# The first router's logits of three token tiles in one stage, their products in turn on three column tiles

## The chip, the cores and the metric

One core of a Trainium2 chip runs the whole program in one launch. The metric is the device time of a run in microseconds; of several runs the median counts. Lower is better.

## The reference

A chunked attention feeds two mixture-of-experts layers, each of which sends a token to the one expert with the largest logit. The change touches the first layer's logits alone.

```
out = softmax(q_c @ k_c.T / 8) @ v_c            # 4 x 8 x 9 chunks of 64 tokens, head size 64
x = out, heads side by side: 2304 tokens x 512
logits = x @ w_gate + modality_bias[modality_id] # 512 x 8: the first router
e = argmax(logits); gate = softmax(logits)[e]
x = gate * (relu(x @ w1[e]) @ w2[e])             # 512 x 1024 x 512, 8 experts
... the second layer: the same with a capacity of 576 tokens per expert
```

## The kernel before, in words

The 2304 tokens are 18 tiles of 128. The program has two parts that overlap a little: attention with the first router, tile by tile, and then 37 expert blocks of up to 128 tokens each, in two layers.

A tile t of attention passes these stages (`tile_ops`, L767 to L829); the letters are used from here on:

- S (TensorE, L778): scores of 8 heads, 16 products of 64 x 64. The two halves of the partitions take turns, so one product reads rows 0 to 63 and writes columns 0 to 63 of the array, the next rows and columns 64 to 127.
- maximum and subtraction (VectorE, L781, L783), exp (ScalarE, L784).
- T (TensorE, L789): four transposes; copy by ScalarE (L791).
- O (TensorE, L798): 16 products with v, in turns as in S.
- the norm (VectorE, three instructions, L804 to L806) writes the tile's rows x into one of four buffers `xr`; a store sends them to HBM (SyncE, L808). A norm so waits until the store of four tiles earlier has left its buffer.
- X (TensorE, L813): four transposes of x; copy by ScalarE into a buffer of `tr` (L815).
- E (TensorE, L821): the router's logits, transposed: four products, with 32 columns of `wgs1` (8 of them experts) as weights and 128 tokens as the moving side, summed in 32 partitions of bank L. Tile j of a group writes partitions 32 j to 32 j + 31, which is column tile j of the array.
- after the last E of a group, once for the group: a copy lt (ScalarE, L825), a transpose F (TensorE, L827), and the addition of the bias into `lg` (VectorE, L828). Groups have 3, 3, 4, 4 and 4 tiles (`LGROUPS`).

The first two groups (six tiles) feed an early routing on VectorE, some 60 small instructions, with ranking (L346, L348), index (L491) and gate (L516) products on TensorE. It chooses the first five blocks. Its table `row1a` tells SyncE which expert's weights to load (`weights`, L553). All 18 tiles feed the second routing, which runs beside the first blocks.

A block gathers its tokens (GpSimd, L617), transposes them (TX, L636), and runs two layers (L649, L678) with float32 split in two parts. The weights are converted into these parts by ScalarE (L597: high part), VectorE and GpSimd (L599: low part). Those of block 0 go into the memory that held the rings of q and k. So their conversion starts only once S of tile 17 is done. The gather of block 0 and its first matmul need no other tile of attention; the stages of tiles 14 to 17 stand around them in the queues.

The order on each engine is fixed when the program is built. A planner takes operations with engine, cost and priority, and simulates their start times; each engine then runs its queue in order. Priority is by tile and stage: tile t's stage d has t + 0.7 d, lower first.

Of the kernel before, what the change touches and what calls it, by code (L numbers as in the profile page):

```python
# [20 lines left out]
P = 128  # L21
NTOK = 2304
NT = NTOK // P
H = 8
HD = 64
D = 512
E = 8
FF = 1024
DC = D // P
# [26 lines left out]
GROUPS = [1, 1] + [2] * 8  # L56
GMAX = 2
RING = 4
LGROUPS = [3, 3, 4, 4, 4]
NB, NX = 3, 4  # L60

MARGIN = 1.0
# [8 lines left out]
class Planner:  # L71
# [14 lines left out]
    def op(self, eng, cost, fn, r=(), w=(), after=(), prio=(MAIN, 0.0), lat=0.1, dma=0.0, name=""):  # L86
        o = Op()
        o.eng = eng if isinstance(eng, dict) else {eng: cost}
        o.fn, o.prio, o.lat, o.dma, o.name = fn, prio, lat, dma, name
        o.margin = 0.0  # L90
        deps = set(after)
        for k in r:
            deps |= set(self.wr.get(k, ()))
        for k in w:
            deps |= set(self.wr.get(k, ())) | set(self.rd.get(k, ()))
        for k in r:
            self.rd.setdefault(k, []).append(o)
        for k in w:
            self.wr[k], self.rd[k] = [o], []
        deps.discard(o)  # L100
        o.deps = deps
        o.n = len(self.ops)
        self.ops.append(o)
        return o
# [54 lines left out]
def kernel(ctx, tc, q, k, v, ids, cap, cst, wg1, bias, w1a, w2a, wg2, w1b, w2b, out):  # L159
    nc = tc.nc  # L160
    V, A, PE, SP, G = nc.vector, nc.scalar, nc.tensor, nc.sync, nc.gpsimd
# [5 lines left out]
    op = plan.op  # L167

    def sb(shape, name, dt=F32, tag=None):
        return cp.tile(shape, dt, name=name, tag=tag or name)  # L170
# [13 lines left out]
    wgs1 = sb([P, DC, 32], "wgs1")  # L184
# [14 lines left out]
    stg1 = [sb([P, DC, FF], f"stg1_{i}") for i in range(2)]  # L199
    stg2 = [sb([P, FC, D], f"stg2_{i}") for i in range(2)]  # L200
    RW = GMAX * H * HD
    big = [sb([P, max(DC * FF, n)], f"big{i}") for i, n in enumerate((RING * RW, RING * RW, RING * GMAX * H * (HD + 1), 6 * 512))]
    qr = big[0][:, 0:RING * RW].rearrange("p (r g a c x) -> p r g a c x", r=RING, g=GMAX, a=4, c=2)
    kr = big[1][:, 0:RING * RW].rearrange("p (r g a c x) -> p r g a c x", r=RING, g=GMAX, a=4, c=2)
    vr = big[2][:, 0:RING * GMAX * H * (HD + 1)].rearrange("p (r g h x) -> p r g h x", r=RING, g=GMAX, h=H)
    tr = big[3][:, 0:6 * 512].rearrange("p (i x) -> p i x", i=6)
    lt = big[3][:, 3072:3200]
    bt1 = big[3][:, 3200:3200 + NT * E].rearrange("p (t e) -> p t e", e=E)
    wv = [None] * 4

    def take(which):
# [5 lines left out]
        return wv[k].rearrange("p (c f) -> p c f", c=(DC, FC)[k // 2])  # L217

    RINGS = [tuple(f"{n}{r}" for r in range(RING)) for n in "qkv"]
    TRS = tuple(f"tr{i}" for i in range(6))  # L220

    WKEYS = ("w1",) + RINGS[0] + RINGS[1], ("w2", "lt", "bt1") + RINGS[2] + TRS

# [530 lines left out]
    where = [(g, j) for g, n in enumerate(GROUPS) for j in range(n)]  # L754
    lwhere = [(n, j) for n in LGROUPS for j in range(n)]
    halves = [slice(0, HD), slice(HD, P)]
# [11 lines left out]
    def tile_ops(t):  # L768
        g, j = where[t]
        r_ = g % RING  # L770
        pr = [(MAIN, t + 0.7 * d - 100) for d in range(5)]
        S = bank[f"A{t % 2}"].rearrange("p (c x) -> p c x", x=HD)
        a, b, c4 = t % 2, 2 + t % 2, 4 + t % 2

        def stA():
            for hc in range(8):
# [24 lines left out]
        rr, x, kx = arr[t % 2], xr[t % NX], f"xr{t % NX}"  # L801
# [7 lines left out]
        X = bank["X"]  # L809
# [2 lines left out]
            for c in range(DC):  # L812
                PE.transpose(X[:, c * P:(c + 1) * P], x[:, c * P:(c + 1) * P], ident)  # L813
        op("PE", 0.44, stD, r=[kx], w=["X"], prio=pr[3], lat=0.25, name=f"X{t}")
        op("A", 0.5, lambda: A.copy(tr[:, c4, :], X), r=["X"], w=[f"tr{c4}"], prio=pr[3], name=f"xt{t}")  # L815
        n, jl = lwhere[t]
        Lb = bank["L"]

        def stE():
            for c in range(DC):  # L820
                PE.matmul(Lb[32 * jl:32 * jl + 32, 0:P], lhsT=wgs1[:, c, :], rhs=tr[:, c4, c * P:(c + 1) * P], start=(c == 0), stop=(c == DC - 1))  # L821
        op("PE", 0.4, stE, r=[f"tr{c4}"], w=["L"], prio=pr[4], lat=0.25, name=f"E{t}")
        if jl == n - 1:
            r, t0 = slice(0, 32 * n), t - jl
            op("A", 0.18, lambda: A.copy(lt[r], Lb[r, 0:P]), r=["L"], w=["lt"], prio=pr[4], name=f"lt{t}")  # L825
            Tv = Lb[:, 256:256 + 32 * n].rearrange("p (a b) -> p a b", b=32)
            op("PE", 0.11, lambda: PE.transpose(Lb[:, 256:256 + 32 * n], lt[r], ident[r, r]), r=["lt"], w=["L"], prio=pr[4], lat=0.25, name=f"F{t}")  # L827
            lgops.append((t, op("V", 0.2, lambda: V.tensor_add(lg[:, t0:t0 + n, :], Tv[:, :, 0:E], bt[:, t0:t0 + n, :]), r=["L", "bt"], prio=pr[4], name=f"lgt{t}")))  # L828
# [36 lines left out]
    for t in range(NT):  # L865
        if where[t][1] == 0 and where[t][0] >= RING:
            load(where[t][0])
        if t == 2:
            op("V", 1.8, prep_small, r=["small"], w=["bt", "bt1"], after=[plan.ops[-1]], prio=(SIDE, 0))
        tile_ops(t)  # L870
# [75 lines left out]
```

## Time and profile before

| what | us |
|---|---|
| median of 3 runs | 620.72 (619.61 to 621.53) |
| the profiled execution: its time | 616.94 |
| its span, first to last instruction | 615.2 |
| TensorE busy | 570.2 |
| VectorE, ScalarE, GpSimd busy | 410.2, 254.8, 268.0 |
| granted clock of TensorE, mean | 0.982 of 2.4 GHz |

The profiled execution is one run, 3.8 us under the median of the timed ones. A row of the timeline merges instructions of one kind that follow each other; xN counts recorded instructions. A float32 product is recorded as two of them. What stands in brackets is idle time of the engine before the row and what ended it. A matmul's recorded duration contains its way through the array, so durations of successive rows overlap; the distance from start to start is what a stage takes.

### The profile page before, as it was taken

The numbers are of one execution on the slowest core, as the hardware profiler recorded it, in microseconds if no ns is written. First come the engines' busy times: TensorE is split into PE (matmuls) and PEld (weight loads), VectorE is DVE, ScalarE is ACT, GpSimd is POOL, SyncE is SP. The second block draws the span as 40 slices with busy tenths as digits, with TensorE's granted clock in tenths as the row PEclk, the third lists the DMA queues.
The fourth block names the chain that finished last, engine by engine and source line by source line (L and its number), as shares of the span: only waits on it lengthen the run. The fifth ranks groups of instructions, "written<-read, shape, count | busy, mean of one in ns | idle before, by whom it ended". The sixth has DMA issues, their size and how long they took to land. (4 is left out here: it accounts for less than half of the span.)

```text
span 615.2 us, 11859 instructions
## 1 busy us (share of the span) xinstructions
PE 570.2 (93%) x4026; PEld 460.6 (75%) x4026; DVE 410.2 (67%) x730; ACT 254.8 (41%) x439; POOL 268.0 (44%) x193
## 2 busy tenths in 40 slices
PE   7999999999999999999897989797999999999991
PEld 6888887778778787878686867686887767786770
DVE  2667675956675466776998885871349897776750
ACT  2444455334343343334344545242426664464430
POOL 3000231354443343433655564182248687645630
PEclk9999999999999999999997999898999999999997
DMA  8977940021423151243144345016565954767000
GB/s 297 409 252 257 385 152 11 0 71 54 138 81 111 39 156 35 58 173 104 69 156 137 114 154 154 31 39 221 166 236 222 336 178 150 259 239 261 14 32 15
DMA packets 44418, 91.78 MB, mean 149 GB/s; under 512 B 7396, under 2 KB 16676, under 8 KB 44208
## 3 DMA queue, kind: packets, MB, share of 16 engines
q1 hardware_dynamic: 38208, 72.13, 33.7%
q0 software_dynamic: 6128, 18.69, 9.0%
q8 instruction: 35, 0.57, 0.4%
q14 instruction: 47, 0.39, 0.2%
HBM read 181.72 MB, written 19.29 MB: 327 GB/s over the span
## 5 line engine op out<-in xcount | busy, mean ns | idle before, releaser
L649 PE MATMUL bankA<-wv,xh 128*128 128x512 f32 x592 | 151.7, 407 | 3.9 <-DVE wv L579 3.0
L696 DVE SCALAR_TENSOR_TENSOR junk<-xr,wgb 128x512 f32<-128x512 f32 x112 | 104.4, 932 | 57.9 <-ACT xr L681 51.9
L649 PEld LDWEIGHTS bankA<-wv,xh 128*128 128x128 f32 x592 | 110.3, 192 | 30.9 <-DVE wv L579 5.6
L579 DVE TENSOR_TENSOR wv<-stg,wv 128x1024 fp32r<-128x1024 f32 (+1 forms) x60 | 125.3, 2139 | 2.6 <-ACT wv L587 2.6
L579 POOL TENSOR_TENSOR wv<-stg,wv 128x1024 fp32r<-128x1024 f32 (+1 forms) x40 | 103.5, 2609 | 40.2 <-DVE wv L584 26.4
L690 POOL TENSOR_TENSOR junk<-xr,wgb 128x512 f32<-128x512 f32 x40 | 60.6, 1519 | 45.9 <-ACT xr L681 45.0
L678 PE MATMUL bankX<-wv,hh 128*128 128x512 f32 x288 | 72.2, 400 | 5.7 <-ACTq L606 3.0
L649 PE MATMUL bankA<-wv,xl 128*128 128x512 f32 x296 | 75.9, 396 | 0.1
L659 ACT ACTIVATE h<-bankA 128x512 f32<-128x512 f32 x74 | 42.3, 593 | 64.7 <-PE bankA L649 64.5
L678 PEld LDWEIGHTS bankX<-wv,hh 128*128 128x128 f32 x288 | 52.7, 188 | 19.4 <-DVE wv L579 4.4
L649 PEld LDWEIGHTS bankA<-wv,xl 128*128 128x128 f32 x296 | 55.2, 188 | 13.8 <-issue 0.6
L587 ACT CAST wv<-stg 128x1024 fp32r<-128x1024 f32 x60 | 59.0, 1049 | 1.2 <-ACT r_ex L364 0.4
L678 PE MATMUL bankL<-wv,hid 128*128 128x512 f32 x216 | 52.8, 399 | 1.4 <-ACTq L606 0.8
L667 PE MATMUL bankO<-ident,h 128*128 128x128 f32 x296 | 45.5, 284 | 7.6 <-ACT h L659 7.2
L691 ACT ACTIVATE junk<-junk 128x512 f32<-128x512 f32 x40 | 25.3, 633 | 58.3 <-POOL junk L690 58.2
L667 PEld LDWEIGHTS bankO<-ident,h 128*128 128x128 f32 x296 | 34.3, 144 | 19.8 <-ACT h L659 15.2
L678 PEld LDWEIGHTS bankL<-wv,hid 128*128 128x128 f32 x216 | 39.8, 188 | 11.1 <-ACTq L606 1.3
L670 DVE TENSOR_TENSOR hl<-bankO,hh 128x512 fp32r<-128x512 f32 x56 | 36.4, 679 | 7.0 <-ACT hh L669 6.9
L670 DVE TENSOR_TENSOR hid<-bankO,hid 128x512 fp32r<-128x512 f32 x18 | 12.1, 686 | 41.6 <-ACT hid L669 36.2
L678 PE MATMUL bankL<-wv,hh 128*128 128x512 f32 x160 | 39.5, 399 | 0.0
L701 POOL DMA_INDIRECT xs<-xr,sidx1b x14 | 15.8, 1126 | 50.0 <-DVEq L606 24.3
L640 DVE TENSOR_TENSOR xl<-bankT,xh 128x512 fp32r<-128x512 f32 x37 | 25.4, 687 | 17.5 <-ACT xh L639 14.3
(203 smaller groups left out, 726.2 us busy)
## 6 DMA issues: line engine op xcount, KB each, us to landing
stg<-in_w1a SPq DMA_DIRECT2D x19, 2048.0 KB
stg<-in_w2a SPq DMA_DIRECT2D x19, 2048.0 KB
stg<-in_w1b SPq DMA_DIRECT2D x18, 2048.0 KB
stg<-in_w2b SPq DMA_DIRECT2D x18, 2048.0 KB
xs<-xr SPq DMA_DIRECT2D x18, 260.0 KB
out<-zero SPq DMA_DIRECT2D x3, 1536.0 KB
big<-in_v SPq DMA_DIRECT2D x8, 520.0 KB
big<-in_q SPq DMA_DIRECT2D x8, 512.0 KB
```

Source lines behind the costliest of these rows:

```text
L579: eng.tensor_sub(lo[:, a:b], s[:, a:b], hi.bitcast(F32)[:, a:b])
L587: A.copy(hi[:, c * FF:(c + 1) * FF], s[:, c * FF:(c + 1) * FF])
L640: op("V", 0.61, lambda: V.tensor_sub(xl[j], Tv, xh[j].bitcast(F32)), r=["T", f"xh{j}"], w=[f"xl{j}"], prio=soon, name=f"xl{i}")
L649: PE.matmul(bank[f"A{n}"], lhsT=lhs[j][:, c, :], rhs=w[:, c, n * 512:(n + 1) * 512], start=(k == 0 and c == 0), stop=(k == 2 and c == DC - 1))
L659: op("A", 0.5, lambda n=n: A.activation(h[:, n, :], bank[f"A{n}"], AF.Relu), r=[f"A{n}"], w=[f"h{n}"], prio=main, name=f"relu{i}")
L667: PE.transpose(On[:, f * P:(f + 1) * P], h[:, n, f * P:(f + 1) * P], ident)
L670: op("V", 0.61, lambda r=r, Ov=Ov: V.tensor_sub(hid[hb][1][:, r, :], Ov, hid[hb][0].bitcast(F32)[:, r, :]), r=[f"O{n}", f"hh{n}{alt}"], w= ...
L678: PE.matmul(Y, lhsT=hid[hb][lhs][:, f, :], rhs=wview(w)[:, f, :], start=(k == 0 and f == 0), stop=(k == 2 and f == FC - 1))
L690: op("G", 1.25, lambda e=e, m=m: G.tensor_mul(junk[m], x1[:, 0:D], wgb[:, e, :]), r=[kx, "wgb"], w=[f"junk{m}"], prio=lp, name=f"lg{i}")
L691: op("A", 0.5, lambda e=e, m=m: A.activation(junk[m], junk[m], AF.Copy, accum_out=x1[:, D + e:D + e + 1]), r=[f"junk{m}"], w=[kx + "A"], p ...
L696: V.scalar_tensor_tensor(junk[0], in0=x1[:, 0:D], scalar=1.0, in1=wgb[:, e, :], op0=ALU.mult, op1=ALU.mult, accum_out=x1[:, D + e:D + e + 1])
L701: G.indirect_dma_start(out=dst, out_offset=bass.IndirectOffsetOnAxis(ap=tab.sidx[:, b:b + 1], axis=0), in_=x1[:, 0:w], in_offset=None, bou ...
```

## The change

- `LGROUPS` becomes six groups of three tiles.
- E is no longer a stage of each tile but of a group: it is issued once, after X of the group's third tile, with all 12 products. The loop over the four chunks is outside, the loop over the three tiles inside, so successive products go to column tiles 0, 1, 2, 0, 1, 2 and so on. The planner's cost for it is 1.1 us, for three former stages of 0.4.
- The transposed x of the three tiles must lie side by side until then: `tr` has seven buffers of 512 where it had six, and three of them, not two, hold transposed x.
- lt, F and the addition come six times, not five, always for three tiles.

```diff
-LGROUPS = [3, 3, 4, 4, 4]
+LGROUPS = [3] * 6
...
-    tr = big[3][:, 0:6 * 512].rearrange("p (i x) -> p i x", i=6)
-    lt = big[3][:, 3072:3200]
+    tr = big[3][:, 0:7 * 512].rearrange("p (i x) -> p i x", i=7)
+    lt = big[3][:, 3584:3712]
...
-        a, b, c4 = t % 2, 2 + t % 2, 4 + t % 2
+        a, b = t % 2, 2 + t % 2
+        n, jl = lwhere[t]
+        c4 = 4 + jl
...
         def stE():
             for c in range(DC):
-                PE.matmul(Lb[32 * jl:32 * jl + 32, 0:P], lhsT=wgs1[:, c, :], rhs=tr[:, c4, c * P:(c + 1) * P], start=(c == 0), stop=(c == DC - 1))
-        op("PE", 0.4, stE, r=[f"tr{c4}"], w=["L"], prio=pr[4], lat=0.25, name=f"E{t}")
+                for k in range(n):
+                    src = tr[:, 4 + k, :]
+                    PE.matmul(Lb[32 * k:32 * k + 32, 0:P], lhsT=wgs1[:, c, :], rhs=src[:, c * P:(c + 1) * P], start=(c == 0), stop=(c == DC - 1))
         if jl == n - 1:
+            op("PE", 1.1, stE, r=[f"tr{4 + k}" for k in range(n)], w=["L"], prio=pr[4], lat=0.25, name=f"E{t}")
```

The planner then puts the stages of attention in another order. In the changed program S is L781, T L792, O L801, X L816, E L825 and F L831.

TensorE in the middle of attention, from T of tile 2 on. Before:

```order
L789 MATMUL bankT<-ident,big_100 128x128 x4
L821 MATMUL bankL<-big_100,wgs_80 32x128 x4
L778 MATMUL bankA_66<-big_98,big_97 64x64 x16
L813 MATMUL bankX<-ident,xr_104 128x128 x4
L798 MATMUL bankO<-big_99,big_100 64x65 x16
```

TensorE, now, a little later: from O of tile 3 to X of tile 3.

```order
L801 MATMUL bankO<-big_99,big_100 64x65 x16
L825 MATMUL bankL<-big_100,wgs_80 32x128 x12
L792 MATMUL bankT<-ident,big_100 128x128 x4
L831 MATMUL bankL<-ident,big_100 128x96
L816 MATMUL bankX<-ident,xr_106 128x128 x4
```

E stood in each tile's turn with 4 products; now it stands in every third turn with 12.

TensorE from the last S (tile 17) to the expert blocks. Before, it is the first row, with X of tile 14 ahead of it:

```order
L778 MATMUL bankA_67<-big_98,big_97 64x64 x16
L798 MATMUL bankO<-big_99,big_100 64x65 x16
L789 MATMUL bankT<-ident,big_100 128x128 x4
L821 MATMUL bankL<-big_100,wgs_80 32x128 x4
L813 MATMUL bankX<-ident,xr_106 128x128 x4
L798 MATMUL bankO<-big_99,big_100 64x65 x16
L789 MATMUL bankT<-ident,big_100 128x128 x4
L821 MATMUL bankL<-big_100,wgs_80 32x128 x4
L636 MATMUL bankT<-ident,xb_107 128x128 x4
L813 MATMUL bankX<-ident,xr_103 128x128 x4
L798 MATMUL bankO<-big_99,big_100 64x65 x16
L821 MATMUL bankL<-big_100,wgs_80 32x128 x4
```

TensorE now, from the last S on:

```order
L781 MATMUL bankA_67<-big_98,big_97 64x64 x16
L792 MATMUL bankT<-ident,big_100 128x128 x4
L816 MATMUL bankX<-ident,xr_105 128x128 x4
L801 MATMUL bankO<-big_99,big_100 64x65 x16
L825 MATMUL bankL<-big_100,wgs_80 32x128 x12
L792 MATMUL bankT<-ident,big_100 128x128 x4
L831 MATMUL bankL<-ident,big_100 128x96
L816 MATMUL bankX<-ident,xr_106 128x128 x4
L801 MATMUL bankO<-big_99,big_100 64x65 x16
L636 MATMUL bankT<-ident,xb_107 128x128 x4
L816 MATMUL bankX<-ident,xr_103 128x128 x4
L801 MATMUL bankO<-big_99,big_100 64x65 x16
```

Both end with TX of block 1 and block 0's first matmul behind what is shown. X of tile 14 (`xr_105`), T of tile 16 and F have moved behind the last S, and three E have become one.

VectorE from the two passes over tile 17's scores on; `wv` is a conversion of block 0's weights, `xr` a norm's last step. Before:

```order
L781 TENSOR_REDUCE amx_125<-bankA_67 128x8
L783 TENSOR_TENSOR big_100<-bankA_67,amx_125 128x512
L804 TENSOR_SCALAR arr_127<-bankO 128x8
L805 RECIPROCAL arr_127<-arr_127 128x8
L806 TENSOR_TENSOR xr_106<-bankO,arr_127 128x512
L599 TENSOR_TENSOR wv_1355<-stg_0_93,wv_1354 128x1024 x2
L804 TENSOR_SCALAR arr_126<-bankO 128x8
L805 RECIPROCAL arr_126<-arr_126 128x8
L806 TENSOR_TENSOR xr_103<-bankO,arr_126 128x512
L599 TENSOR_TENSOR wv_1355<-stg_0_93,wv_1354 128x1024
L640 TENSOR_TENSOR xl_112<-bankT,xh_110 128x512
```

VectorE now, from the same place:

```order
L784 TENSOR_REDUCE amx_125<-bankA_67 128x8
L786 TENSOR_TENSOR big_100<-bankA_67,amx_125 128x512
L807 TENSOR_SCALAR arr_126<-bankO 128x8
L808 RECIPROCAL arr_126<-arr_126 128x8
L809 TENSOR_TENSOR xr_105<-bankO,arr_126 128x512
L599 TENSOR_TENSOR wv_1322<-stg_0_93,wv_1321 128x1024
L807 TENSOR_SCALAR arr_127<-bankO 128x8
L808 RECIPROCAL arr_127<-arr_127 128x8
L809 TENSOR_TENSOR xr_106<-bankO,arr_127 128x512
L599 TENSOR_TENSOR wv_1322<-stg_0_93,wv_1321 128x1024
L832 TENSOR_TENSOR lg<-bankL,bt 128x24
L599 TENSOR_TENSOR wv_1322<-stg_0_93,wv_1321 128x1024
```

Norm 14 (`xr_105`) has come behind the last scores, norm 16 (`xr_103`) now follows only behind the last row shown, and an addition into `lg` stands between the conversions.

SyncE around the first weight loads: `xs<-xr_105` is the store of tile 10. Before:

```order
L808 DMA xs<-xr_104 128x520
L872 DMA wgb<-in_wg 128x4096
L808 DMA xs<-xr_105 128x520
L565 TENSOR_LOAD row1a
L565 ISA x2
L553 ISA
L553 DMA stg_0_93<-in_w1a 128x4x1024
```

SyncE now, at the fourth weight issue:

```order
L566 TENSOR_LOAD row1a
L566 ISA x2
L553 ISA
L553 DMA stg_1_96<-in_w2a 128x8x512
L811 DMA xs<-xr_105 128x520
L811 DMA xs<-xr_106 128x520
```

The store of tile 10 has moved from ahead of the four weight issues to behind them.

## Rows read from the trace of the kernel before

**Rows 1.** The page, engines: busy us (share of span) and recorded instructions

```profile
PE 570.2 (93%) x4026; PEld 460.6 (75%) x4026; DVE 410.2 (67%) x730; ACT 254.8 (41%) x439; POOL 268.0 (44%) x193
```

**Rows 2.** Busy time by stage: length, engines' busy us, granted clock, DMA

```profile
20.00:80.00 60.00, 60.00 (x1138) 51.10 (x1138) 40.09 (x128) 26.27 (x48) 4.61 (x7) 1.00 0.87 319
```

**Rows 3.** Timeline of TensorE, one tile's turn: start us, us, instruction, count

```profile
23.98 1.06 PE L821 MATMUL bankL<-big,wgs 128*32 128x128 f32 x8
24.98 1.15 PE L778 MATMUL bankA<-big,big 64*64 64x64 f32 x32
26.05 0.65 PE L813 MATMUL bankX<-ident,xr 128*128 128x128 f32 x4
...
27.72 0.66 PE L789 MATMUL bankT<-ident,big 128*128 128x128 f32 x4
28.30 1.06 PE L821 MATMUL bankL<-big,wgs 128*32 128x128 f32 x8
```

**Rows 4.** By line, 0 to 95 us: busy us, mean ns, idle before

```profile
L778 PEld LDWEIGHTS bankA<-big,big 64*64 64x64 f32 x576 | 18.3, 134 | 6.5 <-issue 6.3 <-DMA big<-in_v 0.2
...
L821 PE MATMUL bankL<-big,wgs 128*32 128x128 f32 x136 | 18.0, 276 | 0.0
L821 PEld LDWEIGHTS bankL<-big,wgs 128*32 128x32 f32 x136 | 13.5, 109 | 2.6 <-issue 1.7 <-ACT big L784 0.8
```

**Rows 5.** Timeline of TensorE, 24.96 to 25.00 us alone

```profile
24.77 0.27 PE L821 MATMUL bankL<-big,wgs 128*32 128x128 f32 x1
24.98 0.27 PE L778 MATMUL bankA<-big,big 64*64 64x64 f32 x2
```

**Rows 6.** Timeline of TensorE, last S to block 0's first matmul

```profile
78.28 1.15 PE L778 MATMUL bankA<-big,big 64*64 64x64 f32 x32
...
86.28 0.66 PE L813 MATMUL bankX<-ident,xr 128*128 128x128 f32 x4 [0.23 <-DVE xr L806]
...
88.94 0.66 PE L636 MATMUL bankT<-ident,xb 128*128 128x128 f32 x4
89.35 3.98 PE L649 MATMUL bankA<-wv,xh 128*128 128x512 f32 x16
```

**Rows 7.** Timelines of ScalarE (three rows) and VectorE (four) there

```profile
79.48 1.99 ACT L597 CAST wv<-stg 128x1024 fp32r<-128x1024 f32 x2
81.38 0.58 ACT L791 COPY big<-bankT 128x512 f32<-128x512 f32 x1
81.86 0.63 ACT L784 ACTIVATE big<-big 128x512 f32<-128x512 f32 x1
...
79.48 0.69 DVE L781 TENSOR_REDUCE amx<-bankA 128x8 f32<-128x512 f32 x1 [0.74 <-PE bankA L778]
...
81.85 3.35 DVE L599 TENSOR_TENSOR wv<-stg,wv 128x1024 fp32r<-128x1024 f32 x2
85.11 0.15 DVE L804 TENSOR_SCALAR arr<-bankO 128x8 f32<-128x8 f32 x1
...
86.15 1.22 DVE L599 TENSOR_TENSOR wv<-stg,wv 128x1024 fp32r<-128x1024 f32 x1
```

**Rows 8.** Busy time by stage, as rows 2: early routing, and after it

```profile
44.15:68.54 24.39, 24.39 (x467) 20.81 (x467) 20.30 (x83) 11.36 (x21) 1.47 (x4) 1.00 0.82 287
...
68.54:79.40 10.86, 10.86 (x209) 9.32 (x209) 4.98 (x11) 4.46 (x9) 3.13 (x3) 1.00 1.03 390
```

**Rows 9.** Timeline of SyncE's DMA issues: start us, us, instruction

```profile
55.64 0.42 SPq L872 DMA_DIRECT2D wgb<-in_wg  x1
...
66.39 20.19 SPq L808 DMA_DIRECT2D xs<-xr  x6
```

**Rows 10.** Timeline of TensorE: the ranking of all 18 tiles

```profile
105.13 0.23 PE L346 MATMUL bankR<-r_oh,ltb 128*128 128x152 bf16 x1 [0.90 <-DVE r_oh L297]
```

**Rows 11.** A late wait of TensorE, and the stretch behind it (TensorE alone)

```profile
421.43 0.63 PE L636 MATMUL bankT<-ident,xb 128*128 128x128 f32 x4 [3.78 <-DMA xb<-xs,gidx2b]
...
420.00:430.00 10.00, 8.57 (x35) 0.83 0.49 177
```

More of the change, by code (lines that the diff above doesn't have):

```diff
@@ L201 @@
     RW = GMAX * H * HD
-    big = [sb([P, max(DC * FF, n)], f"big{i}") for i, n in enumerate((RING * RW, RING * RW, RING * GMAX * H * (HD + 1), 6 * 512))]
+    big = [sb([P, max(DC * FF, n)], f"big{i}") for i, n in enumerate((RING * RW, RING * RW, RING * GMAX * H * (HD + 1), 7 * 512))]
     qr = big[0][:, 0:RING * RW].rearrange("p (r g a c x) -> p r g a c x", r=RING, g=GMAX, a=4, c=2)
@@ L205 @@
     vr = big[2][:, 0:RING * GMAX * H * (HD + 1)].rearrange("p (r g h x) -> p r g h x", r=RING, g=GMAX, h=H)
-    tr = big[3][:, 0:6 * 512].rearrange("p (i x) -> p i x", i=6)
-    lt = big[3][:, 3072:3200]
-    bt1 = big[3][:, 3200:3200 + NT * E].rearrange("p (t e) -> p t e", e=E)
+    tr = big[3][:, 0:7 * 512].rearrange("p (i x) -> p i x", i=7)
+    lt = big[3][:, 3584:3712]
+    bt1 = big[3][:, 3712:3712 + NT * E].rearrange("p (t e) -> p t e", e=E)
     wv = [None] * 4
@@ L219 @@
     RINGS = [tuple(f"{n}{r}" for r in range(RING)) for n in "qkv"]
-    TRS = tuple(f"tr{i}" for i in range(6))
+    TRS = tuple(f"tr{i}" for i in range(7))
     WKEYS = ("w1",) + RINGS[0] + RINGS[1], ("w2", "lt", "bt1") + RINGS[2] + TRS
@@ L772, in tile_ops @@
         S = bank[f"A{t % 2}"].rearrange("p (c x) -> p c x", x=HD)
-        a, b, c4 = t % 2, 2 + t % 2, 4 + t % 2
+        a, b = t % 2, 2 + t % 2
+        n, jl = lwhere[t]
+        c4 = 4 + jl
+        xT = tr[:, c4, :]
         def stA():
@@ L814, in tile_ops @@
         op("PE", 0.44, stD, r=[kx], w=["X"], prio=pr[3], lat=0.25, name=f"X{t}")
-        op("A", 0.5, lambda: A.copy(tr[:, c4, :], X), r=["X"], w=[f"tr{c4}"], prio=pr[3], name=f"xt{t}")
-        n, jl = lwhere[t]
+        op("A", 0.5, lambda: A.copy(xT, X), r=["X"], w=[f"tr{c4}"], prio=pr[3], name=f"xt{t}")
         Lb = bank["L"]
```

## The prediction

> **What bounds the kernel now.** I read the page first for the shares, then the stages, then the timeline of TensorE through attention and the handover to the expert blocks, and last the queues of VectorE, ScalarE and SyncE there. TensorE is busy 570.2 us, 93% of the span [rows 1]. From 20 to 80 us, which is attention, it is busy all of the 60 us, at the full clock, 2.4 GHz [rows 2]. The page's other engines stay far below that, so the expert blocks are bound by it as well. So time taken from TensorE's queue in attention can reach the end, unless something else becomes late. One tile's turn on TensorE is E, S, X, O, T [rows 3]: E 1.00 us (23.98 to 24.98), S 1.07, X and O together 1.67 (26.05 to 27.72), T 0.58, in all 4.32 us. 17 of the 18 E stand ahead of block 0's first matmul at 89.35 us (136 recorded passes, 8 for an E) [rows 4, 6].
>
> **E alone.** A recorded product of float32 is two passes, so an E of four products is eight. They start 0.113 us apart (24.77 less 23.98, over 7) [rows 3, 5], and 0.21 us lie between the last start and the next stage's first. In the new E a group of three tiles has 24 passes, alternating over three column tiles. Whether those run side by side no row of E can show, since before each E stays on one column tile. The nearest row is S: its products alternate between two tiles of 64 by 64, its first two passes start within one 0.04 us window [rows 5], and 32 passes fit a slot of 1.07 us. Passes one after another, at half of E's 0.113 us for half the columns, would need 32 x 0.057 = 1.81 us. So two tiles run almost wholly side by side there, weight loads included: S's loads last 134 ns each and keep the load path busy 18.3 us for 576 of them, 32 ns apiece [rows 4]. The bounds for a group are then 8 x 0.113 + 0.1 = 1.0 us (three side by side), 12 x 0.118 + 0.1 = 1.5 (only neighbours overlap), 24 x 0.113 + 0.1 = 2.8 (one after another), against 3.0 us for three E before. I take 1.0, since S is the same machinery, and keep the others as rivals. What S leaves open is that its two tiles differ in rows as well as columns, while the three of E read all 128 rows.
>
> The Trainium skill (TensorE: Matmul & The Clock Gate, Part 3: Packing small matmuls) gives 2.38 times for three column tiles of 32 with 512 columns; by that a group would be 2.7 / 2.38 + 0.1, an estimate of 1.24 us, and the forecast 1.2 us later. No run here shows the figure yet.
>
> **The sum on TensorE.** Ahead of block 0 the change takes out 17 E and puts in five groups, and one F more (one transposing product, a fourth of T's slot: 0.14 us; five where four stood): 17 x 1.00 - 5 x 1.00 - 0.14 = 11.9 us. The last group stands inside block 0 where E17 stood, at the same 1.0 us. This is not what is gained, because VectorE and ScalarE have the same work in less time.
>
> **Up to the last S.** Before, S17 starts at 78.28 us [rows 6]. Ahead of it 14 E become four groups, -10.0 us, and X14 has moved behind it, about -0.6 (as T): 67.7 us if nothing waits. VectorE has in a tile's turn two passes over the scores and a norm, about 2.4 us, and the early routing besides: from 44.15 to 68.54 us it is busy 20.30 of 24.39 us [rows 8]. In that stretch TensorE gives up some 4 us, so VectorE would need 20.3 of about 20.4. Going through the new order slot by slot with these durations, X waits for its norm a few tenths at some five places; I put 1.4 us in all (bounds 0.5 and 3). S17 then starts at 69.1 us. DMA loads of q, k, v were ahead by many tiles, and stay so.
>
> **From S17 to block 0.** Here the gain shrinks. Before, 11.07 us pass from S17's start to the first matmul of block 0 (78.28 to 89.35), with one wait of 0.23 us [rows 6]. In the new order TensorE's own work there is S 1.07, three X with O 5.01, two T 1.16, E 1.0, F 0.14, two TX 0.99 (0.58 as T, and 0.41, 88.94 to 89.35): 9.4 us. But the weights' conversion can only begin once S17 has read the rings that it overwrites, and VectorE's queue now has, behind S17: its two passes over the scores (0.69 each), norm 14, a conversion, norm 15, a conversion, lg, a conversion, norm 16; before it had norms 15 and 16 there, and norm 14 lay earlier. Counted from S17's end: scores done at 1.6, norm 14 (1.04, 85.11 to 86.15) at 2.65; the first conversion needs a second cast of ScalarE, which has exp 0.6, cast 1.0, copy 0.6, exp 0.6, cast 1.0 in its queue, so 3.9; two conversions of 1.6 (3.35 for two) and one of 1.2 with norm 15 and lg between them reach 9.4, norm 16 10.45 [rows 7]. Then X16 with O17 1.67, TX 0.41: block 0 starts 12.6 us behind S17's end, 13.7 behind its start. So TensorE waits about 4.3 us in this stretch (for norm 14 ahead of X14, for lt ahead of F, for norm 16 ahead of X16). The gain at block 0 is 89.35 - (69.1 + 13.7) = 6.5 us.
>
> SyncE's queue moves too: the store of tile 10 now stands behind the four weight issues, where it stood ahead. Norm 14 overwrites the same buffer and so waits for that store. Before, stores issued from 66.39 us stood behind 6.3 MB (wgb and two weight loads of 2,048 KB, wgb issued at 55.64) [rows 9]; at the 390 GB/s of this stretch [rows 8] that and the stores and gathers between take some 20 us. wgb is now issued near 50.7, so the store lands near 71 us, and norm 14 wants to start near 71.7. It costs nothing in the forecast; a landing 2 us later would cost 1.3 us.
>
> **Behind block 0.** The first 18-tile ranking waited 0.90 us for VectorE on TensorE [rows 10]; in the new order it stands behind the second layer of block 0, so that wait goes (-0.9), and its index and gate products stand one layer later, ahead of a gather that still has two layers of time. From there the blocks keep their order, and nothing there is tied to absolute time, so an earlier start carries. I give the 0.9 back for waits that I have not found in the reordered blocks 1 to 4.
>
> **Sum.** 6.5 us less. The profiled execution took 616.94 us (span 615.2), 3.8 us under the median of 620.72; I apply the difference to the median: **614.2 us**.
>
> One thing shakes it. A 3.78 us wait for a gather at 421.43 is followed by a stretch in which the granted clock averages 0.83 [rows 11]: part of it at 1.2 GHz, 10 x (1 - 0.83) / 0.5 = 3.4 us, which loses half of that. Whether a wait is answered with the lower level may fall otherwise in a run that starts its blocks earlier: 2 us either way.
>
> **The rivals.**
> - *Only neighbours overlap.* A group is 1.5 us. Four groups ahead of S17 and the last one cost 0.5 each; the fifth hides in the waits of the handover. -6.5 + 2.5 = -4.0: 616.7 us. For it: two passes of one product must follow each other on one column tile, and a strict queue would hold the next tile's behind them. Against it: S starts in pairs from its first pass.
> - *The change doesn't do what it says: column tiles take turns, but one after another.* A group is 2.8 us. +1.8 for the four and the last, 9.0 us, less the 1.4 us of waits that longer groups absorb: -6.5 + 9.0 - 1.4 = +1.1: 621.8 us. For it: the three read the same 128 rows, which no row shows side by side. Against it: S. The Trainium skill (TensorE: Matmul & The Clock Gate, Part 3: Packing small matmuls) says that a weight load overlaps matmuls in flight only where its group of rows differs, which would make this rival of E. The trace disagrees as far as it goes: E's loads, all on the same rows, keep the load path busy 13.5 us within E's 18.0 [rows 4].
> - *Slower: each change of column tile drains the array.* The price is that of a change of stage, 0.21 - 0.113 = 0.1 us: 24 x 0.113 + 12 x 0.1 = 3.9 us a group against 3.0. -6.5 + 5 x 2.9 - 1.4 = +6.6: 627.3 us. It decides from a group of about 2.6 us on, where the sum crosses zero. Against it: S changes tiles 16 times in 1.07 us.
> - *VectorE takes all of the handover.* The store of tile 10, or casts that come late, push norm 14 and all behind it 4 us further: -2.5, 618.2 us.
>
> **How the numbers follow.** Forecast 0.60, neighbours 0.14, one after another 0.14, drain 0.05, handover 0.07. The forecast's own bounds are 611 and 617.5 (waits 0.5 to 3, clock 2, the store). 8 in 10 reaches from 610.5 to 621.5. Faster by over 0.3% (about what a measurement of this kernel can tell from no change) means under 618.86 us: nearly all of the forecast, most of the neighbours, half of the handover, in all 0.71; within 0.3% 0.17; slower, over 622.6, 0.12 (the drain, a third of one after another, and clock).
>
> **What would show it.** E's passes: 24 in about 1.0 us and not 1.5 or 2.8. The last S near 69 us, block 0's first matmul near 83. Between them waits of TensorE for a norm and for lt, together about 4 us, that were 0.23. No wait at the 18-tile ranking. If E's groups take 1.0 us and block 0 still starts after 86 us, the handover was the error; if it starts at 83 and the end gains less than 4 us, it is the blocks or the clock.

## The result, and the profile after

The changed kernel takes 625.16 us (median of 6 runs) against 620.21 us of the kernel before (6 runs) beside it: a ratio of 1.0079, 95% interval 1.0055 to 1.0103. It is slower by 0.8%; the forecast was 614.2 us, 1% faster. Its profiled execution took 622.56 us with a span of 620.8 us. Single executions of one kernel differ here by up to 1%, so times are compared by medians and ratios, and places in the program by the profiles.

The page's engines and the by-line view from 0 to 95 us (count | busy us, mean ns | idle before), which answer to [rows 1] and [rows 4]:

```profile
PE 564.3 (91%) x4027; PEld 455.4 (73%) x4027; DVE 413.8 (67%) x731; ACT 254.1 (41%) x440; POOL 265.9 (43%) x193
...
L825 PE MATMUL bankL<-big,wgs 128*32 128x128 f32 x144 | 6.4, 276 | 0.0
L825 PEld LDWEIGHTS bankL<-big,wgs 128*32 128x32 f32 x144 | 4.8, 109 | 1.0 <-issue 0.9
```

TensorE lost 5.9 us of busy time and the span grew by 5.6. The logits alone fell from 18.0 busy us to 6.4. The timeline of TensorE, one group and what follows it, and then a window of 0.06 us at the group's start:

```profile
27.61 1.07 PE L825 MATMUL bankL<-big,wgs 128*32 128x128 f32 x24
28.61 0.66 PE L792 MATMUL bankT<-ident,big 128*128 128x128 f32 x4
...
27.61 0.31 PE L825 MATMUL bankL<-big,wgs 128*32 128x128 f32 x3
```

Twenty-four passes fit the slot of 1.00 us (27.61 to 28.61) in which one tile's eight stood before [rows 3], and three of them start within the window: the three column tiles run side by side, pass by pass. The handover, TensorE from the last S to block 0's first matmul (in brackets: idle before, and who ended it):

```profile
70.81 1.15 PE L781 MATMUL bankA<-big,big 64*64 64x64 f32 x32
72.47 0.66 PE L792 MATMUL bankT<-ident,big 128*128 128x128 f32 x4 [0.52 <-ACT big L787]
74.58 0.66 PE L816 MATMUL bankX<-ident,xr 128*128 128x128 f32 x4 [1.45 <-DVE xr L809]
...
81.45 0.63 PE L816 MATMUL bankX<-ident,xr 128*128 128x128 f32 x4 [1.09 <-DVE xr L809]
...
83.50 3.98 PE L649 MATMUL bankA<-wv,xh 128*128 128x512 f32 x16
```

Block 0 starts 5.85 us earlier than before (83.50 against 89.35, [rows 6]). That gain is still there at block 2's layer 2, which starts 7.2 us earlier (125.99 against 133.20). Block 4's layer 2 starts 4.6 us **later** (163.38 against 158.76), and from there the lag stays between 4.6 and 6.3 us to the end. So the changed kernel falls back by 11.8 us between blocks 2 and 4. TensorE's timeline there, with VectorE's and GpSimd's (POOL) at the first wait and VectorE's at the second:

```profile
125.99 3.97 PE L678 MATMUL bankL<-wv,hh 128*128 128x512 f32 x16
...
131.66 1.07 PE L491 MATMUL bankR<-r_sv,r_OH 128*128 128x25 bf16 x36
132.58 0.78 PE L516 MATMUL bankR<-r_sv,r_OH 128*128 128x75 bf16 x18
136.13 1.11 PE L667 MATMUL bankO<-ident,h 128*128 128x128 f32 x4 [2.77 <-DVEq L606]
136.90 6.23 PE L649 MATMUL bankA<-wv,xh 128*128 128x512 f32 x16
...
155.32 0.97 PE L636 MATMUL bankT<-ident,xb 128*128 128x128 f32 x4 [3.38 <-DVE xl L640]
155.94 5.34 PE L649 MATMUL bankA<-wv,xh 128*128 128x512 f32 x16
...
132.58 0.72 DVE L696 SCALAR_TENSOR_TENSOR junk<-xr,wgb 128x512 f32<-128x512 f32 x1 [0.78 <-ACT xr L681]
133.34 2.13 DVE L696 SCALAR_TENSOR_TENSOR junk<-xr,wgb 128x512 f32<-128x512 f32 x1
135.40 0.68 DVE L670 TENSOR_TENSOR hl<-bankO,hh 128x512 fp32r<-128x512 f32 x1
...
133.64 1.27 POOL L690 TENSOR_TENSOR junk<-xr,wgb 128x512 f32<-128x512 f32 x1
...
152.56 2.09 DVE L696 SCALAR_TENSOR_TENSOR junk<-xr,wgb 128x512 f32<-128x512 f32 x1
154.58 0.68 DVE L640 TENSOR_TENSOR xl<-bankT,xh 128x512 fp32r<-128x512 f32 x1
```

Two waits are new, 2.77 and 3.38 us. Both are for a step on VectorE (hl, with the branch of the conversion behind it; xl) that stands behind logits passes of an expert block (L696). The index and gate products of the second routing (L491, L516) now stand together behind block 2's layer 2, where before they stood ahead of it. And each wait is followed by a stretch at a lower granted clock (stretch, then length, busy us, granted clock, DMA share, GB/s):

```profile
130.00:140.00 10.00, 7.23 (x73) 0.75 0.07 27
140.00:150.00 10.00, 10.00 (x43) 0.91 0.36 108
150.00:160.00 10.00, 6.62 (x29) 0.83 0.17 53
```

Between the two levels, 1.2 and 2.4 GHz, these are 10 x (0.25 + 0.09 + 0.17) / 0.5 = 10.2 us at 1.2 GHz. A part of them lies in the waits, where it costs nothing. The rows behind the waits tell the cost: the two layers 1 took 6.23 and 5.34 us, where 3.98 is usual [rows 6], which is 3.6 us, and the transposes ahead of them some 0.6 more, so about 4.2 us. The index and gate products, which before lay ahead of this stretch, take 1.7 us in it; they are work that was put off, not lost. Waits of 6.15, clock 4.2 and products 1.7, less a wait of 0.33 us that the kernel before has there, make 11.7 of the 11.8 us. Why both waits came is left to the experiments.

### The profile page after: what moved, and what is told of

Its sections match the earlier page's. It is cut to its first block, busy times and chain, and to the rows that moved or that the text cites. A ratio compares the mean times of both kernels' runs of the same rounds, so it can differ in the third digit from the quotient of the medians.

```text
span 620.8 us, 11861 instructions
## 1 busy us (share of the span) xinstructions
PE 564.3 (91%) x4027; PEld 455.4 (73%) x4027; DVE 413.8 (67%) x731; ACT 254.1 (41%) x440; POOL 265.9 (43%) x193
## 5 line engine op out<-in xcount | busy, mean ns | idle before, releaser
L649 PE MATMUL bankA<-wv,xh 128*128 128x512 f32 x592 | 156.0, 416 | 3.9 <-DVE wv L579 2.9
L696 DVE SCALAR_TENSOR_TENSOR junk<-xr,wgb 128x512 f32<-128x512 f32 x112 | 102.4, 914 | 60.0 <-ACT xr L681 54.5
L649 PEld LDWEIGHTS bankA<-wv,xh 128*128 128x128 f32 x592 | 113.5, 198 | 31.7 <-DVE wv L579 5.5
L579 DVE TENSOR_TENSOR wv<-stg,wv 128x1024 fp32r<-128x1024 f32 (+1 forms) x60 | 128.3, 2190 | 3.4 <-ACT wv L587 3.4
L678 PE MATMUL bankX<-wv,hh 128*128 128x512 f32 x288 | 73.7, 406 | 5.6 <-ACTq L606 3.1
```

The source lines that it names most:

```text
L579: eng.tensor_sub(lo[:, a:b], s[:, a:b], hi.bitcast(F32)[:, a:b])
L649: PE.matmul(bank[f"A{n}"], lhsT=lhs[j][:, c, :], rhs=w[:, c, n * 512:(n + 1) * 512], start=(k == 0 and c == 0), stop=(k == 2 and c == DC - 1))
L678: PE.matmul(Y, lhsT=hid[hb][lhs][:, f, :], rhs=wview(w)[:, f, :], start=(k == 0 and f == 0), stop=(k == 2 and f == FC - 1))
L696: V.scalar_tensor_tensor(junk[0], in0=x1[:, 0:D], scalar=1.0, in1=wgb[:, e, :], op0=ALU.mult, op1=ALU.mult, accum_out=x1[:, D + e:D + e + 1])
```

## The experiments

"Order" below is the sequence in which the planner emits steps to the engines. Some kernels take part of that order from a table of step numbers instead of the planner's choice; the steps themselves are the same.

**1. The changed order without the overlap** (new_order): the kernel before, with the changed kernel's order from block 0's layer 2 to block 4's (154 step numbers in the table).

```
+FIRST = 401
+ORDER = [
...
+            if FIRST <= step < FIRST + len(ORDER):
+                o = self.ops[ORDER[step - FIRST]]
```

> The kernel before, each tile's logits by themselves, with one thing of the changed kernel: from block 0's layer 2 on the next 154 steps stand in the changed kernel's order. Block 0 still starts near 89.4. Theory 1 (the order alone makes the waits): TensorE waits about 2.8 us for the transposes of block 2's second half or block 3 and about 3.4 us at TX6, each followed by a stretch at half clock, and the time is 628 to 632 us. Theory 2 (the early start makes them): no wait over 1 us there and 619 to 622 us. Should only the two together make them, this kernel and the one with the old order are both without the waits: 620 and 614 us.

Measured: 628.78 us against 619.59 of the kernel before, ratio 1.0149 (1.0112 to 1.0185). TensorE's waits from 83 us on (what waited, releaser: us in total, times, longest us):

```profile
PE bankT L651 <- DVE xl L655: 3.4, 1, 3.4
...
PE bankO L682 <- DVEq L621: 2.0, 1, 2.0
```

The order alone makes both waits, the first of 2.0 us and not 2.8, and costs 9 us, as theory 1 said.

**2. The old order with the overlap** (old_order, and old_order_2, which begins one block later): the changed kernel with the table the other way round, 156 and 120 steps in the order of before.

> The changed kernel, but from block 0's layer 2 on the next 156 steps stand in the order of the kernel before, so that the index and gate products of the second routing stand before block 2's layer 2 again, and TX5 before block 3's layer 2. Everything up to block 0 is as in the changed kernel. Theory 1 (the new order made the two waits of 2.77 and 3.38 us, and these the two stretches at half clock): block 0 starts near 83.5, neither wait is there, block 4's layer 2 starts about 5 us before the kernel before (near 153.5 instead of 163.4), and the time is 613 to 616 us. Theory 2 (the second routing's vector work runs late in absolute time, so that any earlier start of the blocks meets it, in whichever order): waits of the same sum turn up at other instructions between 120 and 160, and the time is 621 to 626 us.

> As the run with the old order, but the old order begins one block later, at block 1's layer 2: the second routing's ranking stays behind block 0's layer 2, where the changed kernel has it, and 120 steps from there stand as in the kernel before. It tells the ranking's place from that of the later products. Theory 1 (what the first run with the old order lost was the ranking alone, 1.48 us of wait for VectorE and the clock behind it): block 0's layer 2 starts near 101, no wait over 1 us up to block 4's layer 2, which starts near 153.5, and 613 to 616 us. Theory 2 (the second routing is late in absolute time): its index products, now before block 2 again, wait 2 us or more near 124 to 128, block 4's layer 2 starts at 157 or later, and the time is 617 to 621 us.

Measured: 619.25 us, ratio 0.9985 (0.9959 to 1.0011), and 621.38 us, ratio 1.0033 (1.0001 to 1.0066). Neither gives back the gain at block 0, so theory 1 is not enough: old_order fell between the two forecasts, and old_order_2 has the waits that theory 2 named, with a time 0.4 us above its range. TensorE's timeline of old_order (first two rows) and of old_order_2:

```profile
104.79 0.28 PE L361 MATMUL bankR<-r_oh,ltb 128*128 128x152 bf16 x1 [1.48 <-DVE r_oh L312]
...
106.09 4.78 PE L693 MATMUL bankL<-wv,hh 128*128 128x512 f32 x16
```

```profile
123.31 0.45 PE L504 MATMUL bankR<-r_sv,r_OH 128*128 128x25 bf16 x12 [2.04 <-DVE r_sv L310]
124.93 0.49 PE L504 MATMUL bankR<-r_sv,r_OH 128*128 128x25 bf16 x12 [1.16 <-DVE r_OH L310]
126.53 0.49 PE L504 MATMUL bankR<-r_sv,r_OH 128*128 128x25 bf16 x12 [1.11 <-DVE r_OH L310]
...
128.47 5.46 PE L662 MATMUL bankA<-wv,xh 128*128 128x512 f32 x16
```

In old_order the ranking ahead of block 0's layer 2 waits for r_oh, which VectorE finishes at nearly the absolute time of before (its ranking: 105.13, [rows 10]), and block 0's layer 2 starts at 106.09 instead of 100.95. From block 2's layer 1 on (112.58, before 112.54) this execution runs in step with the kernel before. In old_order_2 the index products wait 4.3 us in three pieces for their operands. So the second routing is late on VectorE in the old order as well.

Not all of it is the routing. Block 0 did not start near 83.5 as expected, but at 85.63 and 85.50, though up to there the program is the changed kernel's. In both executions norm 14 waited for the store of tile 10, whose buffer it overwrites, TensorE for the norm (2.25 and 3.49 us), and the stages behind ran at the lower clock: O took 2.00 us instead of 1.15. VectorE in old_order:

```profile
73.93 0.69 DVE L824 TENSOR_TENSOR xr<-bankO,arr 128x512 f32<-128x512 f32 x1 [0.83 <-DMA xs<-xr]
```

So 2.1 of the 5.1 us by which old_order's block 0 reached its layer 2 late were lost ahead of block 0.

**3. One planner number** (cost_1_0).

```
-            op("PE", 1.1, stE, r=[f"tr{4 + k}" for k in range(n)], w=["L"], prio=pr[4], lat=0.25, name=f"E{t}")
+            op("PE", 1.0, stE, r=[f"tr{4 + k}" for k in range(n)], w=["L"], prio=pr[4], lat=0.25, name=f"E{t}")
```

> The changed kernel with one number changed: the planner's cost of the grouped logits is 1.0 instead of 1.1. The planner then puts the second routing's products before block 2's layer 2 again, and it also starts block 0 ahead of the last tiles' attention (its first layer stands before the attention of tile 16 is finished). Theory 1: no waits of 2.8 and 3.4 us between 120 and 160, and 612 to 617 us; the first number of the range if the earlier layer 1 of block 0 fills waits of the handover, the last if it only moves them. Theory 2: 621 to 626 us.

Measured: 613.03 us against 619.59, ratio 0.9899 (0.9861 to 0.9937), within theory 1's range: the best of all, faster than both kernels. TensorE and VectorE, the last group's logits to block 0's layer 2; then the two VectorE rows of the changed kernel:

```profile
80.40 3.98 PE L649 MATMUL bankA<-wv,xh 128*128 128x512 f32 x16
...
96.97 0.23 PE L346 MATMUL bankR<-r_oh,ltb 128*128 128x152 bf16 x1 [0.73 <-DVE r_oh L297]
...
99.08 3.98 PE L678 MATMUL bankL<-wv,hh 128*128 128x512 f32 x16
...
92.28 0.18 DVE L832 TENSOR_TENSOR lg<-bankL,bt 128x24 f32<-128x24 f32 x1 [0.15 <-DVEq L606]
...
96.61 0.30 DVE L297 TENSOR_TENSOR r_oh<-r_eq,r_wm 128x144 bf16<-128x144 f32 x1
```

```profile
91.58 0.18 DVE L832 TENSOR_TENSOR lg<-bankL,bt 128x24 f32<-128x24 f32 x1 [6.49 <-PE bankL L831]
...
102.30 0.31 DVE L297 TENSOR_TENSOR r_oh<-r_eq,r_wm 128x144 bf16<-128x144 f32 x1
```

Here r_oh follows the last logits after 4.3 us, in the changed kernel after 10.7: there it stands, among other things, behind all three parts of a weight conversion, here behind one. The ranking comes 8.2 us earlier than before, together with the blocks (block 4's layer 2: 152.17, 6.6 us earlier), and the two waits are absent.

**4. The order of cost_1_0 from block 1's layer 1 on, with an earlier second routing** (early_rank, early_rank_2): the changed kernel up to block 1's layer 1, then 186 steps in the order of cost_1_0; early_rank_2 puts block 3's transposes TX3 back inside block 1's layer 1. These are the first steps of early_rank (482 is r_oh, 483 the ranking, 373 and 374 the two parts of block 1's layer 1, 425 is TX3, which early_rank_2 has behind 375):

```
+FIRST = 360
+ORDER = [
+    398, 399, 344, 345, 425, 373, 478, 479, 349, 484, 348, 480, 481, 485, 350, 351, 482, 353, 352, 354, 483,
+    375, 374, 486, 503, 355, 395, 487, 377, 516, 376, 488, 491, 356, 517, 489, 426, 518, 490, 492, 427, 400,
...
```

> The changed kernel up to block 1's layer 1; from there 186 steps stand as in the version with the planner's cost 1.0: the one-hot of the second routing (r_oh) behind the first of the three conversion parts on VectorE, the ranking inside block 1's layer 1, the routing's other steps before block 0's logits, and the index and gate products before block 2's layer 2. The attention and the start of block 0 are the changed kernel's. Theory 4 (the earlier block 0 pays only if the second routing's vector work comes forward with it; the changed kernel put the ranking behind block 0's layer 2, 1.5 us later than before): block 0 starts near 83.5, the ranking runs at 97 to 99 instead of 106.6, no wait over 1.5 us between 100 and 160, block 4's layer 2 at 152.5 to 154, and 612.5 to 616 us. Theory 5 (the gain of the version with the cost 1.0 comes from its attention and block 0's start at 80.4): the ranking's gain is small and the time is 618 us or more.

> As the run early_rank with one step put back: block 3's transposes TX3, which stood there ahead of block 1's layer 1 and waited 2.40 us for VectorE, stand inside it behind the ranking. Theory 4 (the changed kernel's earlier block 0 pays if the second routing's vector work comes forward with it): block 0 starts at 83.5 to 85.5, the ranking runs at 98 to 101, no wait over 1.5 us between 90 and 160, block 4's layer 2 starts at 153 to 155.5, and the time is 613 to 616.5 us. Theory 6 (the gain of 6.6 us of the version with cost 1.0 needs its attention's order as well, since only there does the last tile's data reach VectorE early enough): a wait of 1.5 us or more turns up again at another instruction and the time is 617.5 us or more.

Measured: early_rank 618.54 us, ratio 0.9978 (0.9954 to 1.0002). By its time this is theory 5, but the trace shows other reasons. Block 0 started at 85.00, as norm 14 waited 1.69 us for the store. And the mixed order had put TX3 where it waits for VectorE, and a stretch at the lower clock follows:

```profile
96.32 0.65 PE L652 MATMUL bankT<-ident,xb 128*128 128x128 f32 x4 [2.40 <-DVE xl L656]
96.73 5.52 PE L665 MATMUL bankA<-wv,xh 128*128 128x512 f32 x16
```

With that one step put back, early_rank_2: 615.18 us against 619.39, ratio 0.9924 (0.9893 to 0.9955), within theory 4's range. Its ranking:

```profile
99.11 0.23 PE L362 MATMUL bankR<-r_oh,ltb 128*128 128x152 bf16 x1 [1.33 <-DVE r_oh L313]
...
101.62 3.97 PE L694 MATMUL bankL<-wv,hh 128*128 128x512 f32 x16
```

Block 4's layer 2 starts at 154.72, 4.0 us earlier than before. Against the changed kernel (1.0079) this is 1.5% from the order between block 1's layer 1 and block 5 alone, with the order of attention untouched. All 186 steps moved together; which of them the gain needs is not shown beyond the ranking's earlier place.

**5. The reverse** (late_rank): cost_1_0 up to block 1's layer 1, then 179 steps in the changed kernel's order (the same kind of table).

> The version with the planner's cost 1.0 up to block 1's layer 1; from there 179 steps stand as in the changed kernel, the ranking behind block 0's layer 2 and the second routing's index and gate products behind block 2's. Block 0 still starts near 80.4. Theory 4: the waits of 2.8 and 3.4 us near 131 to 155 are back with their stretches at half clock, and the time is 621 to 626 us. Theory 5: 613 to 616 us.

Measured: 617.75 us, ratio 0.9976 (0.9950 to 1.0002), between the two. The waits are back at the same instructions, but smaller, and the granted clock stays at 1.00 from 130 to 160 us:

```profile
133.38 0.66 PE L683 MATMUL bankO<-ident,h 128*128 128x128 f32 x4 [1.31 <-DVEq L622]
...
148.55 0.66 PE L652 MATMUL bankT<-ident,xb 128*128 128x128 f32 x4 [1.98 <-DVE xl L656]
```

So theory 4 has the place right and not the size: with block 0 another 3 us earlier, the same order costs 0.8% and not 1.5%. Each of these two differences is uncertain by about 0.4 to 0.5%.

**6. The clock behind the waits** (busy_waits): dummy products in both waits of the changed kernel; they are extra work, and nobody reads their results.

```
+            if l == 1 and not early:
+                for _ in range(44):
+                    PE.matmul(bank["X"][:, 0:P], lhsT=onb, rhs=onb, start=True, stop=True)
...
+            if i == 6:
+                for _ in range(52):
+                    PE.matmul(bank["L"][:, 0:P], lhsT=onb, rhs=onb, start=True, stop=True)
```

> The changed kernel with two packs of small bf16 products on ones whose results nobody reads, 44 behind the gate products of the second routing and 52 ahead of TX6, so that TensorE works through the two waits of 2.77 and 3.38 us. The planner's costs and the order are those of the changed kernel. Theory 1 (the stretches at 1.2 GHz behind the waits, 6.8 and 3.4 us long, follow from TensorE standing still): the waits are filled, granted clock 1.00 between 130 and 160, layers 1 of blocks 4 and 6 take 3.97 us each instead of 6.23 and 5.34, and the time is 619 to 621.5 us. Theory 3 (the clock falls for another reason): the stretches stay and the time is 625 us or a little more.

Measured: 618.12 us against 618.86, ratio 0.9999 (0.9969 to 1.0028), a little below the range of theory 1; 0.8% or 4.9 us less than the changed kernel, by doing more. (The second slow layer 1 is block 5's, not block 6's as the expectation has it.) TensorE's timeline, and the stretch (as above):

```profile
133.68 2.62 PE L519 MATMUL bankX<-onb 128*128 128x128 bf16 x44
136.61 0.66 PE L673 MATMUL bankO<-ident,h 128*128 128x128 f32 x4 [0.32 <-DVEq L609]
137.03 3.98 PE L655 MATMUL bankA<-wv,xh 128*128 128x512 f32 x16
...
130.00:140.00 10.00, 9.68 (x125) 1.00 0.08 30
```

The waiting itself stays, now filled; the lower clock is gone. So these drops follow from TensorE standing still, and the split is about 6 us of waits and 4 to 5 us of clock. (A further drop at block 15 is also absent from this execution, so a little of the 4.9 us may come from there.)

**7. What the overlap is worth** (no_overlap): cost_1_0 with the first tile of each group computed twice more (8 products, 16 recorded passes), which makes a group nearly as long as three tiles apart: 2.74 us from start to start, against 3.0.

```
-            for c in range(DC):
-                for k in range(n):
+            for c, k in [(c, k) for c in range(DC) for k in range(n)] + 2 * [(c, 0) for c in range(DC)]:
+                if True:
```

> The version with the planner's cost 1.0, and each group's first tile computed twice more behind the 24 products, 16 more products on one column tile, so that a group of three takes about the 3.0 us that three tiles take apart; order and results are the same. It measures what the three column tiles working side by side are worth where the order is good. Theory 1 (TensorE bounds the attention): six groups by 2.0 us are 12 us, of which the handover's waits hide 2 to 5: block 0 starts 7 to 10 us later than with the cost 1.0 (near 88 to 90 instead of 80.4), and the time is 619 to 624 us. Rival (the gain of the version with cost 1.0 is the order of its attention and blocks, the overlap is worth little): 613 to 616 us.

Measured: 620.02 us, ratio 1.0008 (0.9982 to 1.0035), within the range; against cost_1_0 1.1%, some 6.8 us. Block 0 starts at 86.26, 5.9 us later than there and not the 7 to 10 expected. In this order no gain over the kernel before is left without the overlap, so there all of it is the overlap's.

**8. Whether taking turns matters** (tile_by_tile): the two loops of the group exchanged.

```
-            for c in range(DC):
-                for k in range(n):
+            for k in range(n):
+                for c in range(DC):
```

> The changed kernel with the two loops of the grouped logits exchanged: eight passes of one tile, then eight of the next, then of the third, on the same three column tiles; nothing else moves. Theory A (passes overlap only with a neighbour in the queue that works on another column tile, so taking turns is what makes the overlap): a group takes about 2.7 us instead of 1.0, and 6 groups cost up to 10 us more, of which the waits of the handover hide a part: 628 to 634 us. Theory B (the array takes work for each column tile as it comes, and the order in the queue doesn't matter): a group stays near 1.0 us and the time at 625 us.

Measured: 626.97 us, ratio 1.0109 (1.0070 to 1.0149), which cannot be told from the changed kernel's 1.0079. Both theories missed the group's length:

```profile
27.39 2.00 PE L825 MATMUL bankL<-big,wgs 128*32 128x128 f32 x24
29.32 0.66 PE L792 MATMUL bankT<-ident,big 128*128 128x128 f32 x4
```

The slot is 1.93 us, between 1.00 in turns and 3.0 apart: the next tile starts while part of the one before is still to come, but only at the two seams. By the slot, taking turns is about half of the overlap.

**9. Groups of three alone** (groups_of_three): the kernel before with six groups, no turns.

```
-LGROUPS = [3, 3, 4, 4, 4]
+LGROUPS = [3] * 6
```

> The kernel before with six groups of three instead of 3, 3, 4, 4, 4: each tile's logits still by themselves on their own column tile, no turns. The planner puts the ranking ahead of block 1's layer 1 here and the index products before block 1's layer 2, earlier than in any of the other kernels. TensorE's work is the 18.0 us of logits as before, with one more transpose of a group. Theory: without the overlap block 0 starts where it did (89 to 90), and an early second routing alone gives nothing, as TensorE had no wait over 1 us there: 617.5 to 621 us. Rival (the early routing is itself what gains, and the overlap adds little): 613 to 616 us.

Measured: 625.84 us, ratio 1.0105 (1.0068 to 1.0141). Both missed: the planner's order for this kernel has an early ranking (101.12), yet block 0 starts at 91.97, and a wait stands at block 3's transposes, with the clock at 0.87 and 0.79 in the two stretches of 10 us behind 130:

```profile
138.15 1.12 PE L667 MATMUL bankO<-ident,h 128*128 128x128 f32 x4 [2.85 <-ACT h L659]
```

Here an early routing without the earlier block 0 gained nothing, and a reorder by the planner, with its own wait and drop of the clock, cost 1% by itself.

## Why the prediction was wrong

- **E alone: right.** A group takes 1.00 us, the bound it chose. Three tiles on the same 128 rows do the work of 3.0 us in 1.00, loads included (4.8 us of load path for 144). The Trainium skill (TensorE: Matmul & The Clock Gate, Part 3: Packing small matmuls) gives 2.38 times for three column tiles with 512 columns, and lets weight loads overlap matmuls only across different groups of rows. The measurement decides: with 128 columns it is 3.0 times, and the rule on loads does not hold for this shape. The rivals of a slower overlap fall with it.
- **Up to the last S: the waits were undersized.** S17 starts at 70.81, not 69.1. Three waits of 0.39, 0.47 and 1.99 us stand ahead of it, 2.9 us against the 1.4 put down and inside the bounds of 0.5 and 3. The longest is F's, for the copy lt, where the prediction put waits of X for a norm; in early_rank's execution, with the same attention, F does not wait and S17 starts at 68.16.
- **From S17 to block 0: near, with some luck.** 12.7 us instead of 13.7; waits of 0.52, 1.45 and 1.09, in all 3.1 us instead of 4.3. Block 0 at 83.50 against a forecast of 82.8, a gain of 5.85 against 6.5. In this execution norm 14 does not wait for the store of tile 10. But the estimate that the store lands near 71 us was too early: norm 14 does wait for it in old_order, old_order_2, early_rank, early_rank_2, cost_1_0 and late_rank, 0.22 to 1.72 us, and runs on at 72.97 to 74.11. In the first four, whose attention is the changed kernel's, block 0 starts at 84.22 to 85.63. The rival of a handover held up by the store is in part true there.
- **Behind block 0: this step failed.** The prediction took from the shares of the whole span that TensorE alone bounds the blocks. Behind block 0 VectorE, with the second routing, is as busy. Of the kernel before (stretch, length, then busy us of PE, PEld, DVE, ACT and POOL, granted clock, DMA share, GB/s):

```profile
100.00:110.00 10.00, 9.10 (x62) 7.46 (x61) 9.82 (x25) 4.92 (x8) 2.40 (x1) 1.00 0.01 2
110.00:120.00 10.00, 10.00 (x47) 7.97 (x45) 9.31 (x26) 4.86 (x10) 4.08 (x4) 1.00 0.00 0
```

  In the changed kernel the ranking's wait did go:

```profile
106.61 0.24 PE L346 MATMUL bankR<-r_oh,ltb 128*128 128x152 bf16 x1
```

  But it went because the ranking was put behind block 0's layer 2, 1.5 us later than before [rows 10] while the blocks ran 5.9 us ahead, and the prediction counted that as a gain of 0.9 us. Three statements of it were wrong. "The blocks keep their order": they did not between blocks 2 and 4; the index and gate products went behind block 2's layer 2 and TX5 behind block 3's. That the products had time to spare: their gather had, but the steps that stand behind them in the queues of VectorE and TensorE had not. And "nothing there is tied to absolute time": the last logits reached `lg` 5.8 us earlier (91.58 against 97.36), as block 0 did, but r_oh only 2.5 us earlier (102.30 against 104.78); the rest went in VectorE's queue. An allowance of 0.9 us stood where 10.5 us were lost, from 5.85 us ahead at block 0 to 4.6 behind at block 4's layer 2: mainly 6.15 us of waits and about 4.2 of clock.
- **The clock: right in kind, mis-sized.** It was held for 2 us either way; each new wait of about 3 us was followed by a drop, in all about 4.2 us.
- **The rivals.** None names what cost the time; all of them asked about TensorE's array and the handover. "Slower" had 0.12, and none of its cases was a wait in the blocks. The prediction's own test did name the place: block 0 near 83 and a gain under 4 us at the end means the blocks or the clock, and it is both.

What stays open: why the order costs less (0.8%) where block 0 starts at 80.4 than where it starts at 83.5; only that the waits are smaller there and the clock holds is shown. At block 15 the changed kernel has a further drop of the clock behind a 3.1 us wait that before has without one; it costs 1.4 us and was not tried. And what share of the two waits comes from the slow logits passes of VectorE (last section) is not shown: the kernel before has such passes too, of up to 1.66 us between 119 and 160 us, and TensorE waits 0.34 us at most there.

## What to carry to other kernels

An earlier start pays only if every chain that joins later moves with it: find what the next stage takes from another engine's queue and by how much *that* comes earlier, before the gain is carried to the end. Where a planner orders the work, compare its order stage by stage far behind the edited place, and try a few values of the new step's cost: here 1.0 instead of 1.1 turned a loss of 0.8% into a gain of 1.0%. A wait that TensorE cannot avoid may be worth filling with idle products, since the clock behind it can cost nearly as much as the wait (here about 4.2 us behind 6.15).

## What the runs showed of the hardware

- Three float32 products of 128 x 32 weights over 128 columns, on three column tiles and the same rows, run side by side in the time of one: 24 passes in 1.00 us. In turns they overlap wholly; queued tile after tile they overlap only in part (1.93 us).
- TensorE's granted clock fell behind waits of 2.77 and 3.38 us (changed kernel), 2.40 (early_rank) and 2.00 (new_order), and in old_order behind two waits of 1.60 and 1.48 us that follow each other closely (block 0's layer 2: 4.78 us instead of 3.98). It held at 1.00 behind waits of 1.31 and 1.98 (late_rank) and of 3.05 (kernel before, at 304.52). So the length of one wait alone does not tell. It held where the waits were filled with small products.
- A logits pass of VectorE (L696) takes 0.69 us, but 2.13 and 2.09 us in the two new waits, where GpSimd multiplies beside it (1.27 us, row at 133.64). In both kernels' profiles no pass without GpSimd work beside it was clearly longer than 0.69, while beside it passes took from 0.69 to 2.62 us. The Trainium skill (Trainium Architecture — The Big Picture, What this means for kernel authors) says that these two engines contend for a shared port which one of them locks. The two long passes agree: 0.69 + 1.27 = 1.96 us, an estimate for a pass that has to wait for GpSimd's whole product, is near them. The passes of 0.69 us beside GpSimd's work show that it does not come every time.
